# A fixed task table for the attention stage, with other engines for some tasks and the k and v tails in two tiles

## The chip, the cores and the metric

The kernel runs on one core of a Trainium2 chip. A core has five engines that run their own instruction streams and wait for each other through semaphores: TensorE (PE in the profile, with its weight loads as PEld), VectorE (DVE), ScalarE (ACT), GpSimd (POOL) and SyncE (SP). All but a few DMA transfers are issued by SP, in the order of its stream. The metric is the device time of one execution in microseconds (us).

## The reference

Three stages follow each other. The first is attention over B=4, H=8, S=576, D=64 with a second, linear read-out that is mixed in by a gate:

```python
scores = scale * np.matmul(q, k.transpose(0, 1, 3, 2))
scores = np.where(causal, -1000000000.0, scores)
a = np.exp(scores - scores.max(-1, keepdims=True))
a /= a.sum(-1, keepdims=True) + 1e-09
local = np.matmul(a, v)
q_p = phi(q)                      # where(q > 0, q, exp(q) - 1) + 1
mem_out = einsum(q_p, M_prev) / (einsum(q_p, z_prev) + 1e-06)
attn = g * mem_out + (1 - g) * local          # g = sigmoid(beta) per head
```

Then a gated MLP (512 to 1536 and back) and a second MLP (512 to 2048 and back) run over the 2304 tokens. Inputs and outputs are float32.

## The kernel before

Attention is cut into 16 pairs of heads: for each of the 4 batches 4 pairs, each written by one call of `Attention.pair(b, n)`. A pair's rows of q, k and v are four chunks of 128 and a tail of 64 rows. Of a pair, PE transposes k (`tk`, L793), q (`tq`, L804) and the tails of k and q (`tm`, L799); ScalarE or VectorE copy the results out of PSUM (L697, tiles `K` and `S`); PE makes the scores (`s`, L914 and, for the tail rows, L948); VectorE masks them and takes the row minima (L928, L955); ScalarE takes the exponentials (L935, L966); VectorE makes the row factors `r` (L991, L996); GpSimd or VectorE scale the rows (L1007 on GpSimd, L1009 on VectorE, in place in tile `a`); PE transposes them (`t`, L1023, L1045, L1062); they are copied out (tile `R`), and the product `av` (L1087, L1095) ends the pair. Its result goes to DRAM (`xs`, L1121). The read-out of phi(q) runs beside it (`e`, `p`, `nrm`: L822 to L857).

The tails of k and of v of a whole batch lie in one tile, `kv`: v in its partitions 0 to 63, k in 64 to 127, in two buffers, so that one batch's tails can be loaded while the other's are in use. `tm` transposes a whole `kv` block, both halves, and uses the columns that came from k. `av` multiplies a whole `kv` block with a row block whose other half is zero.

Between the pairs stand weight conversions for the next stage (L1160 to L1246) and, from about 85 us on, 24 early products of the gated MLP (`mm`, L1563), for which VectorE and ScalarE need little. PE also runs products on zeros (`idle`, L1517 and L1587), which fill time in which it would wait; there are 9 at the start and 30 (`SPIN`) that are tasks of the plan.

All this is recorded as tasks of a `Plan` with an engine, a cost, what they depend on and which buffers they use. `choose` makes a task with two possible engines; the string `CHOICE` has a digit for each. `order()` then simulates the engines with the costs and takes, on each engine, the ready task with the lowest number in the table `RANK`. The tasks are written in the order that comes out, and each engine's stream is that order with the other engines left out. The simulation makes VectorE and GpSimd wait for each other by rules of its own (`port`, `ends`, `shut`). If a plan has a `table`, `by_table()` is used instead: it lists the tasks in their final order, and costs and rules play no part. The plan of the main stage (`TABLE`) is of that kind already.

The main stage follows on every engine. Its first products (L1749, 144 matmuls) use early tiles `xw`; then come the chains (L1815 and others). It reads `xs` back (`xr`, L1686) and the weight numbers that attention stored (`num`, read at L1327).

Of the kernel before, what the change touches and what calls it, by code (L numbers as in the profile page):

```python
# [19 lines left out]
P = 128  # L20
# [33 lines left out]
    "0100010001010100010001010011110101101010000010010000000000100000000010101011100000011011111010100010"  # L54
    "1100000001010001000000100000010010000101001110011001001010101010110010000101010100101011111010001000"
    "0111010101100000100010100110000111100010100000010101000001011111100001010000100010001000011000110010"
    "0001100001000100011010011000000010001000010100011000001100000010100000010010000000000010100100110000"
    "0010100000101111010100001010000000001010001100101011010111101000001100001111000010100101001011011101"
)
RANK = (  # L60
# [474 lines left out]
def c_tr(n):  # L535
    return 109 * n
# [1647 lines left out]
```

## Time and profile before

| | |
|---|---|
| median of 3 runs | 1011.12 us (1010.63 to 1011.39) |
| the profiled execution | 1011.15 us |
| its span, first to last instruction | 1009.4 us |
| last attention product ends, main stage starts on PE | 247.98 us |
| PE busy over the span | 986.7 us (98%) |
| DVE, ACT, POOL busy over the span | 799.1, 622.9, 129.9 us |
| mean granted TensorE clock | 0.99 of 2.4 GHz |

About 1.75 us of the execution lie outside the span. GpSimd has work in the attention stage alone. A busy PE is not a PE at its peak: the ends of matmuls are modelled, and at half clock it counts as busy too, so the granted clock has to be read beside it.

### The profile page before, as it was taken

The page shows a single profiled execution, that of the slowest core. Times are in us where ns is not written, and L with a number is a line of the kernel's source. Part 1 is how long each engine was busy: PE and PEld are TensorE (multiplying, and loading weights), DVE is VectorE, ACT ScalarE, POOL GpSimd, SP SyncE. Part 2 cuts the span into 40 slices and gives each one's busy share as a digit, 9 for nine tenths or more (in the row PEclk, how much of TensorE's full clock was granted, in tenths as well). Part 3 has the DMA queues.
Part 4 walks back from the last instruction along what each step waited for, and adds up shares of the span by engine and source line. Part 5 has one row for each costly group of instructions (what it writes and reads, how often), then busy time and mean ns, then how long its engine had stood idle before and what let it go on. Part 6 is the DMA issues. An engine that isn't in the chain of part 4 may idle for free.

```text
span 1009.4 us, 17905 instructions
## 1 busy us (share of the span) xinstructions
PE 986.7 (98%) x6546; PEld 929.0 (92%) x6546; DVE 799.1 (79%) x1648; ACT 622.9 (62%) x1287; POOL 129.9 (13%) x170
## 2 busy tenths in 40 slices
PE   7989999999999999999999999999999998999997
PEld 6667777778999999999999999999999998999997
DVE  4989988983888778787768887687788867987983
ACT  4889888863665656656355645577877854454541
POOL 3354657751000000000000000000000000000000
PEclk9989999999999999999999999999999999999999
DMA  8747444222843555657997863125455895544441
GB/s 191 193 117 209 115 123 111 77 73 81 276 134 113 170 178 178 223 187 278 359 348 252 302 225 125 42 88 194 158 193 194 286 343 174 170 155 132 147 135 43
DMA packets 161848, 178.91 MB, mean 177 GB/s; under 512 B 68064, under 2 KB 133088, under 8 KB 161760
## 3 DMA queue, kind: packets, MB, share of 16 engines
q1 hardware_dynamic: 140702, 158.33, 48.6%
q10 hardware_dynamic: 21058, 19.44, 6.3%
q8 instruction: 51, 0.84, 0.3%
q14 instruction: 37, 0.30, 0.1%
HBM read 114.82 MB, written 62.91 MB: 176 GB/s over the span
## 4 chain that ended last, share of the span: by engine, by line
PE 89%; DVE 6%; DMA 2%; ACT 1%; issue 1%; POOL 0%; SPq 0%; ACTq 0%; DVEq 0%
PE mm L1815 39%; PE mm L1990 16%; PE mm L1899 15%; PE av L1095 3%; PE s L914 3%; PE mm L1749 2%; PE t L1045 2%; PE mm L1563 2%; DVE a L928 2%; PE av L1087 1%; PE s L948 1%; DMA rg<-h2s 1%; PE t L1062 1%; PE idle L1587 1%; DMA h2s<-r 1%
## 5 line engine op out<-in xcount | busy, mean ns | idle before, releaser
L1815 PE MATMUL mm<-xw 128*128 128x384 f32 x1944 | 346.4, 334 | 0.6 <-DVE r L1846 0.6
L1815 PEld LDWEIGHTS mm<-xw 128*128 128x128 f32 x1944 | 337.7, 188 | 1.0 <-DVE r L1846 1.0
L1990 PE MATMUL mm<-xw 128*128 128x256 f32 x1296 | 162.6, 284 | 3.1 <-DVE xw L1968 3.1
L1990 PEld LDWEIGHTS mm<-xw 128*128 128x128 f32 x1296 | 159.2, 193 | 3.3 <-DVE xw L1968 3.3
L1899 PE MATMUL mm<-xw 128*128 128x384 f32 x864 | 150.1, 334 | 0.0
L1899 PEld LDWEIGHTS mm<-xw 128*128 128x128 f32 x864 | 149.8, 188 | 0.0
L1967 ACT CAST xw<-rg 128x768 fp32r<-128x768 f32 x72 | 58.5, 833 | 50.5 <-DVE rg L1963 15.1
L935 ACT ACTIVATE a<-a,mn 128x256 f32<-128x256 f32 (+3 forms) x128 | 70.6, 555 | 10.6 <-DVE mn L928 10.3
L1968 DVE TENSOR_TENSOR xw<-rg,xw 128x768 fp32r<-128x768 f32 x72 | 67.4, 952 | 2.4 <-ACT xw L1967 2.3
L1007 POOL TENSOR_SCALAR a<-a,r,one 128x128 f32<-128x128 f32 (+4 forms) x79 | 60.5, 775 | 40.0 <-DVE r L996 20.4
L1815 PE MATMUL mm<-xw,wh 128*128 128x384 f32 x324 | 64.8, 334 | 0.0
L1837 ACT COPY mm<-mm 128x384 f32<-128x384 f32 x54 | 25.1, 465 | 63.7 <-PE mm L1815 63.6
L928 DVE CUSTOM_DVE_ANT_0 a<-s,mask 128x384 f32<-128x384 f32 (+3 forms) x128 | 55.1, 483 | 6.3 <-PE s L914 6.2
L1815 PEld LDWEIGHTS mm<-xw,wh 128*128 128x128 f32 x324 | 56.9, 188 | 0.0
L697 ACT COPY R<-t 128x384 f32<-128x384 f32 (+2 forms) x104 | 47.5, 501 | 15.0 <-PE t L1045 9.5
L1095 PE MATMUL av<-R,vn 128*64 128x320 f32 (+3 forms) x384 | 48.0, 379 | 0.4 <-ACT R L697 0.4
L1095 PEld LDWEIGHTS av<-R,vn 128*64 128x64 f32 x384 | 28.1, 137 | 21.4 <-ACT R L697 1.0
L1698 ACT CAST xw<-h 128x768 fp32r<-128x768 f32 x36 | 29.7, 835 | 28.1 <-DMA h<-hs 17.3
L1701 DVE TENSOR_TENSOR xw<-h,xw 128x768 fp32r<-128x768 f32 x36 | 33.7, 952 | 14.5 <-ACT xw L1698 14.5
L1349 DVE TENSOR_TENSOR wp<-wp 128x256 f32<-128x256 f32 x104 | 42.5, 421 | 1.6
L914 PE MATMUL s<-K,S 64*128 64x256 f32 (+3 forms) x256 | 39.8, 445 | 0.0
L1231 DVE TENSOR_TENSOR xw<-wp,xw 128x768 fp32r<-128x768 f32 x36 | 33.9, 952 | 4.3 <-ACT xw L1229 4.0
(182 smaller groups left out, 1660.7 us busy)
## 6 DMA issues: line engine op xcount, KB each, us to landing
h2s<-r SPq DMA_DIRECT2D x48, 384.0 KB, 3.8
rg<-h2s ACTq DMA_DIRECT2D x72, 256.0 KB, 3.5
park<-pk SPq DMA_DIRECT2D x27, 512.0 KB, 3.0
hs<-h SPq DMA_DIRECT2D x33, 384.0 KB, 5.2
h<-hs SPq DMA_DIRECT2D x33, 384.0 KB, 4.5
xr<-xs SPq DMA_DIRECT2D x24, 384.0 KB, 3.5
rw<-in_moe_w_out_dram SPq DMA_DIRECT2D x16, 512.0 KB, 4.7
rw<-in_moe_w_in_dram SPq DMA_DIRECT2D x16, 512.0 KB, 4.6
```

What stands on the lines that cost most here:

```text
L697: copy(dst(), src())
L914: nc.tensor.matmul(out[h][:, at_[c]:at_[c] + kl[c]], st["S"][halves[h], c * P:(c + 1) * P], st["K"][halves[h], 0:kl[c]], start=True, stop= ...
L928: nc.vector.tensor_tensor_reduce(a, st[f"s{h}{tag}"][:, at_[c]:at_[c] + kl[c]], self.mask0[:, 512 - kl[c]:512], -0.125, 3.0e38, ALU.add, A ...
L935: nc.scalar.activation(a, a, AF.Exp, bias=mn[:, o:o + 1], scale=-1.0, accum_out=sm[:, o:o + 1])
L1007: eng.tensor_scalar(a, a, r, self.one, op0=ALU.mult, op1=ALU.mult)
L1095: nc.tensor.matmul(o[rg][halves[h], c0:c1], V, r, start=False, stop=i == len(terms[rg]) - 1, tile_position=(0, h * 64), skip_group_check=True)
L1349: return lambda: fn(f32(W(o, o + 1)), f32(W(x, x + 1)), f32(W(y, y + 1)))
L1815: nc.tensor.matmul(o, S["k"](k, pw, j), x[k]["at"](px, j), start=begin and not (i or j), stop=j == 1 and i == 2, skip_group_check=True)
L1899: nc.tensor.matmul(o, u["k"](pw, m), h["at"](px, j), start=(p == 0 and j == 0 and n == 0), stop=(p == F1 // 2 - 1 and j == 1 and n == 2), ...
L1967: t = add_act(256 * (b - a), lambda: nc.scalar.copy(dst(j)[:, 0], R(a, b)), deps, [*i_r, i_x[j]])
L1968: return add_dve(256 * (b - a), lambda: nc.vector.tensor_sub(dst(j)[:, 1], R(a, b), f32(dst(j)[:, 0])), [t], [*i_r, i_x[j]])
L1990: nc.tensor.matmul(o, dst(j)[:, px, i, g - 1 - 3 * j], u["k"](w, pw), start=b + i + q == 0 and k in OPEN, stop=b == 3 and i == 1 and q == ...
```

## The change

The attention plan gets a table `FIRST` (1434 numbers, one for each task that is not a transfer in flight) and no `RANK`, so that its order too is written out and nothing is simulated. `CHOICE` has other digits, so some tasks stand on another engine. `kv` with two buffers becomes `kt` (k's tails, zeros in partitions 0 to 63) and `vt` (v's tails, zeros in 64 to 127) with one buffer each; the memory is the same. Three costs and one `port` mark change as well; with a table they decide nothing in this program.

```diff
-    (RANK, 1554 numbers)
+FIRST = (
+    121, 91, 90, 104, 115, 107, 116, 141, 111, 112, 139, 119, 83, 123, 94, 124, 144, 86, 145, 110, 142, 103, 146,
...
 CHOICE = (
-    "0100010001010100010001010011110101101010000010010000000000100000000010101011100000011011111010100010"
+    "1101000111001010000001011101000000000000100011000010010111101100000001001010001000000001101000001010"
...
-        for tags, n in ((("kn", "qn", "vn", "K", "S"), 3), (("zb", "MZ", "a4", "P", "kv", "qz"), 2),
+        for tags, n in ((("kn", "qn", "vn", "K", "S"), 3), (("zb", "MZ", "a4", "P", "qz"), 2), (("kt", "vt"), 1),
...
+        nc.vector.memset(self.kt[0][0:64], 0.0)
+        nc.vector.memset(self.vt[0][64:128], 0.0)
...
-                dma("tails", [690], lambda: tails(self.kv[i_kv.slot], self.k, dn), uses=[i_kv]),
+                dma("tails", [690], lambda: tails(self.kt[i_kt.slot], self.k, dn), uses=[i_kt]),
...
-            held["t_v"] = dma("tails", [690], lambda: tails(self.kv[i_kv.slot], self.v, up), uses=[i_kv])
+            held["t_v"] = dma("tails", [690], lambda: tails(self.vt[i_vt.slot], self.v, up), uses=[i_vt])
...
-            for o, x in (0, self.kv[i_kv.slot]), (128, self.qz[i_qz.slot]):
+            for o, x in (0, self.kt[i_kt.slot]), (128, self.qz[i_qz.slot]):
...
-                            V = st["vn"][:, kc, h] if kc < 4 else self.kv[i_kv.slot][:, n, h]
+                            V = st["vn"][:, kc, h] if kc < 4 else self.vt[i_vt.slot][:, n, h]
...
-                    slow={"PE": (4600, 2)}, turn=TURN, choice=CHOICE, rank=RANK)
+                    slow={"PE": (4600, 2)}, turn=TURN, choice=CHOICE, table=FIRST)
```

The number of instructions of each kind is the same on PE and SP. On VectorE 4 `e<-qn` (L824) and 4 `e<-p,zb` (L836) less stand in the attention stage, and on GpSimd 4 more of each (L822, L836); GpSimd's whole list grows by 18 instructions. In the changed kernel most lines have numbers that are 7 lower (L1749 there is L1742).

**The tails, on SP.** Before, the load of v's tails of the first batch stands behind a weight load and in front of M:

```order
L1160 DMA raw_374<-in_moe_w_gate_dram 128x4x256
L726 DMA kv_0_183<-in_v_dram 64x8x64
L730 DMA MZ_0_187<-in_M_prev_dram 64x4x64 x2
L730 DMA MZ_1_188<-in_M_prev_dram 64x4x64 x2
L711 DMA kn_1_176<-in_k_dram 128x4x64 x2
```

Now, with the v rows of the first pair moved ahead of it:

```order
L704 DMA vn_0_178<-in_v_dram 128x4x64 x2
L723 DMA MZ_0_187<-in_M_prev_dram 64x4x64 x2
L719 DMA vt_0_184<-in_v_dram 64x8x64
L1153 DMA raw_624<-in_moe_w_gate_dram 128x4x256
L704 DMA qn_651<-in_q_dram 128x4x64 x2
```

The load writes `kv_0_183` before and a tile of its own now. **The tails, on PE**, where the fourth tail transpose (`tm`) of the first batch stands. Before:

```order
L948 MATMUL s40_391<-K_294 128x288
L948 MATMUL s41_398<-K_294 128x288
L948 MATMUL s40_404<-K_395 128x288
L799 MATMUL tm_412<-ident_60,kv_0_183 128x128
L799 MATMUL tm_412<-ident_60,qz_0_185 128x128
```

Now:

```order
L856 MATMUL tp_412<-ident_60,p_263 128x128 x4
L859 MATMUL tp4_417<-ident_60,p_263 64x128
L786 MATMUL tk_424<-ident_60,kn_2_177 128x128 x4
L792 MATMUL tm_431<-ident_60,kt_0_183 128x128
L792 MATMUL tm_431<-ident_60,qz_0_185 128x128
```

The transpose reads `kt`, which no load of v writes. **The start, on ACT's queue** (the first pair's second halves of q and k, and q's tail, 128x1x64). Before:

```order
L636 DMA bb_220<-in_beta_dram 128x8
L723 DMA qn_225<-in_q_dram 128x1x64
L711 DMA qn_225<-in_q_dram 128x4x64
L711 DMA kn_0_175<-in_k_dram 128x4x64
L639 ACT_TABLE_LOAD
```

Now:

```order
L629 DMA bb_220<-in_beta_dram 128x8
L704 DMA qn_230<-in_q_dram 128x4x64
L704 DMA kn_0_175<-in_k_dram 128x4x64
L716 DMA qn_230<-in_q_dram 128x1x64
L632 ACT_TABLE_LOAD
```

The tail moved behind the two halves. **The start, on PE**, up to the first scores. Before:

```order
L1517 MATMUL idle_206<-still_131 64x128 x9
L1587 MATMUL idle_240<-still_131 64x128 x11
L804 MATMUL tq_261<-ident_60,qn_225 128x128 x4
L1587 MATMUL idle_240<-still_131 64x128 x5
L793 MATMUL tk_288<-ident_60,kn_0_175 128x128 x4
L1587 MATMUL idle_240<-still_131 64x128 x4
L914 MATMUL s02_301<-K_294,S_274 128x384
```

Now:

```order
L1510 MATMUL idle_206<-still_131 64x128 x9
L1580 MATMUL idle_226<-still_131 64x128 x4
L797 MATMUL tq_234<-ident_60,qn_230 128x128 x4
L786 MATMUL tk_241<-ident_60,kn_0_175 128x128 x4
L1580 MATMUL idle_226<-still_131 64x128 x5
L907 MATMUL s02_265<-K_259,S_253 128x384
```

Eleven of the zero products left this place and stand later. **The second tail block, on PE**: `t4` transposes the scaled tail rows of the second pair that comes to it. Before:

```order
L914 MATMUL s13_768<-K_437,S_645 128x512
L799 MATMUL tm_787<-ident_60,kv_1_184 128x128
L799 MATMUL tm_787<-ident_60,qz_1_186 128x128
L793 MATMUL tk_792<-ident_60,kn_2_177 128x128 x4
L804 MATMUL tq_800<-ident_60,qn_652 128x128 x4
L1023 MATMUL t4_830<-ident_60,a4_0_181 128x128 x4
```

Now:

```order
L907 MATMUL s13_709<-K_353,S_660 128x512
L1580 MATMUL idle_226<-still_131 64x128 x5
L786 MATMUL tk_740<-ident_60,kn_1_176 128x128 x4
L1580 MATMUL idle_226<-still_131 64x128 x4
L797 MATMUL tq_756<-ident_60,qn_748 128x128 x4
L1016 MATMUL t4_761<-ident_60,a4_1_182 128x128 x4
```

Nine zero products stand in this place now. The scaling that `t4` waits for (L1009 of `a4`, 128x576) is the 135th instruction of VectorE's stream before and the 120th now.

## Rows read from the trace of the kernel before

**Rows 1.** The page's head: span, and busy time of each engine.

```profile
span 1009.4 us, 17905 instructions
PE 986.7 (98%) x6546; PEld 929.0 (92%) x6546; DVE 799.1 (79%) x1648; ACT 622.9 (62%) x1287; POOL 129.9 (13%) x170
```

**Rows 2.** Busy time by stretch: us, engines (instructions), granted clock, DMA share, GB/s.

```profile
0.00:25.00 25.00, 19.00 (x119) 15.54 (x120) 12.32 (x45) 10.02 (x28) 9.77 (x31) 0.95 0.89 191
25.00:75.00 50.00, 45.02 (x299) 32.40 (x299) 44.27 (x152) 44.71 (x121) 20.34 (x28) 0.89 0.61 156
75.00:250.00 175.00, 173.14 (x1355) 132.27 (x1352) 144.46 (x482) 133.83 (x388) 99.83 (x112) 1.00 0.41 113
250.00:1009.40 759.40, 749.53 (x4778) 748.80 (x4777) 598.04 (x971) 434.32 (x753) 0.00 (x0) 1.00 0.57 193
```

**Rows 3.** PE's order in time: start, us, line, instructions, idle before.

```profile
14.40 0.33 PE L799 MATMUL tm<-ident,kv 128*128 128x128 f32 x1
...
24.14 0.45 PE L799 MATMUL tm<-ident,kv 128*128 128x128 f32 x1 [5.03 <-DMA kv<-in_v_dram]
```

**Rows 4.** SP's order in time, transfers issued at 17 to 19 us.

```profile
17.56 0.82 SPq L1160 DMA_DIRECT2D raw<-in_moe_w_gate_dram  x1
18.48 0.64 SPq L726 DMA_DIRECT2D kv<-in_v_dram  x1
```

**Rows 5.** Busy time by stretch, in and behind PE's two long waits.

```profile
18.70:23.90 5.20, 0.41 (x2) 0.00 (x0) 1.27 (x8) 1.32 (x4) 0.84 (x2) 0.87 1.21 231
23.90:29.20 5.30, 5.06 (x18) 3.44 (x18) 3.00 (x13) 1.85 (x4) 0.45 (x1) 0.50 0.81 167
50.80:54.60 3.80, 0.29 (x4) 0.06 (x2) 3.80 (x16) 3.80 (x13) 2.42 (x3) 0.82 0.89 190
54.60:60.30 5.70, 5.70 (x23) 5.02 (x24) 4.50 (x18) 3.65 (x10) 1.75 (x3) 0.52 0.33 76
```

**Rows 6.** PE's order in time at the second wait.

```profile
54.59 1.12 PE L1023 MATMUL t<-ident,a 128*128 128x128 f32 x4 [3.51 <-DVE a L1009]
```

**Rows 7.** VectorE: the scaling waited for, and its work up to there by stretch.

```profile
54.02 0.91 DVE L1009 TENSOR_SCALAR a<-a,r 128x576 f32<-128x576 f32 x2
...
0.00:54.60 54.60, 43.62 (x279) 32.31 (x279) 39.35 (x136) 36.95 (x101) 20.46 (x44) 0.93 0.83 193
```

**Rows 8.** The start in time: ACT's queue, then PE.

```profile
1.21 1.15 ACTq L723 DMA_DIRECT2D qn<-in_q_dram  x1
2.39 0.39 ACTq L711 DMA_DIRECT2D qn<-in_q_dram  x1
...
8.25 1.31 PE L1587 MATMUL idle<-still 128*64 128x128 f32 x10
9.49 0.66 PE L793 MATMUL tk<-ident,kn 128*128 128x128 f32 x4
10.07 1.09 PE L1587 MATMUL idle<-still 128*64 128x128 f32 x8
11.09 2.43 PE L914 MATMUL s<-K,S 64*128 64x384 f32 x16
```

**Rows 9.** Groups by line and shape, 0 to 248 us: busy, mean ns, idle before.

```profile
L824 DVE TENSOR_SCALAR e<-qn 128x576 f32<-128x576 f32 x11 | 4.8, 440 | 1.7 <-DMA qn<-in_q_dram 1.7
L836 DVE TENSOR_TENSOR e<-p,zb 128x512 f32<-128x512 f32 x8 | 5.5, 686 | 0.0
L822 POOL TENSOR_SCALAR e<-qn 128x576 f32<-128x576 f32 x5 | 10.7, 2137 | 4.8 <-issue 2.3 <-DVE nrm L844 1.7 <-DMA qn<-in_q_dram 0.8
L836 POOL TENSOR_TENSOR e<-p,zb 128x512 f32<-128x512 f32 x8 | 10.6, 1329 | 22.3 <-DVE nrm L851 12.1 <-DVE p L831 10.1
```

**Rows 10.** VectorE's row factors by shape, 0 to 248 us, and both shapes' spread.

```profile
L991 DVE SCALAR_TENSOR_TENSOR r<-sum,OGP 128x4 f32<-128x4 f32 x16 | 6.3, 392 | 0.9 <-ACT a L935 0.8
L991 DVE SCALAR_TENSOR_TENSOR r<-sum,OGP x32: 147/164/1092, 19.6 to 229.0; 128x4 f32<-128x4 f32 x16, 128x5 f32<-128x5 f32 x16
```

**Rows 11.** PE's order in time where the main stage starts.

```profile
247.98 25.23 PE L1749 MATMUL mm<-xw 128*128 128x384 f32 x144
```

More of the change, by code (lines that the diff above doesn't have):

```diff
@@ L53 @@
 CHOICE = (
-    "0100010001010100010001010011110101101010000010010000000000100000000010101011100000011011111010100010"
[L55 to L58, printed above, removed]
-)
-RANK = (
[76 rows of a table removed]
+    "1101000111001010000001011101000000000000100011000010010111101100000001001010001000000001101000001010"
+    "1010000001001000001000000000101010000000000100000111000011010000111110010000000000010100101110110010"
+    "0001001100010000000110010001000011000011001010101001100010010010100010000001011101010010010000001011"
+    "0101011101000011001000011100001000011000000001011110110000010011101010010101100010010110100000010000"
+    "0010111110101000100011101000011100100001010001000001010011000000010010000001011100100110101111000001"
+)
+FIRST = (
[70 rows of a table added]
 TABLE = (
@@ L303, with __init__ @@
     RELEASE = 90
-    def __init__(self, start=None, over=None, lat=None, slow=None, stay=0, turn=0, keep=False, choice="", rank=(), table=()):
+    def __init__(self, start=None, over=None, lat=None, slow=None, stay=0, turn=0, keep=False, choice="", table=()):
         self.slow, self.stay, self.turn, self.keep = slow or {}, stay, turn, keep
@@ L309, in __init__ @@
         self.tasks, self.caps, self.taken, self.start = [], {}, {}, start or {}
-        self.choice, self.chosen, self.rank, self.table = choice, 0, rank, table
+        self.choice, self.chosen, self.table = choice, 0, table
         self.opened = None
@@ L322, in add @@
     def add(self, eng, dur, prio, fn, deps=(), uses=(), lat=0, behind=None, port=False, form=0, by=None):
-        if self.rank:
-            prio = self.rank[len(self.tasks)]
         t = {"eng": eng, "port": port, "form": form, "dur": dur + (self.over.get(eng, 0) if self.over else 0), "prio": (prio, len(self.tasks)), "fn": fn, "uses": list(dict.fromkeys(uses)),
@@ L615, in __init__ @@
         self.a4 = [ac.tile([P, 640], F32, name=f"a4_{i}") for i in range(2)]
-        self.kv, self.qz, self.MZ = (
-            [ac.tile([P, NP, 2, D], F32, name=f"{x}_{i}") for i in range(2)] for x in ("kv", "qz", "MZ"))
+        self.kt, self.vt, self.qz, self.MZ = (
+            [ac.tile([P, NP, 2, D], F32, name=f"{x}_{i}") for i in range(n)]
+            for x, n in (("kt", 1), ("vt", 1), ("qz", 2), ("MZ", 2)))
+        nc.vector.memset(self.kt[0][0:64], 0.0)
+        nc.vector.memset(self.vt[0][64:128], 0.0)
         self.one = ac.tile([P, 1], F32, name="one")
@@ L620, in __init__ @@
         for i in range(2):
-            nc.vector.memset(self.kv[i][0:64], 0.0)
             for h in range(2):
@@ L732, in pair @@
         if n == 0:
-            self.batch = {"z": pl.inst("zb"), "M": pl.inst("MZ"), "k": pl.inst("kv"), "q": pl.inst("qz")}
+            self.batch = {"z": pl.inst("zb"), "M": pl.inst("MZ"), "k": pl.inst("kt"), "v": pl.inst("vt"), "q": pl.inst("qz")}
         held = self.batch
-        i_z, i_M, i_kv, i_qz = (held[x] for x in "zMkq")
+        i_z, i_M, i_kt, i_vt, i_qz = (held[x] for x in "zMkvq")
         i_K, i_S, i_P = pl.inst("K"), pl.inst("S"), pl.inst("P")
@@ L809, in pair @@
         t_tk = add("PE", c_tr(4), "tk", tk, l_k, [i_k, i_tk, i_K])
-        t_tm = add("PE", c_tr(2), "tm", tm, t_kt, [i_kv, i_qz, i_tm, i_K])
+        t_tm = add("PE", c_tr(2), "tm", tm, t_kt, [i_kt, i_qz, i_tm, i_K])
         t_tq = add("PE", c_tr(4), "tq", tq, l_q[:2], [i_q, i_tq, i_S])
@@ L866, in tp @@
             nc.tensor.transpose(t[0:64, 0:128], p[:, 8], self.ident)
-        t = choose("min", [("POOL", c_pool(576) + 60, lambda: f_min(nc.gpsimd), False),
+        t = choose("min", [("POOL", 2080, lambda: f_min(nc.gpsimd), False),
                            ("DVE", c_dve(576), lambda: f_min(nc.vector), True)], l_q, [i_q, i_e])
@@ L996, in f_inv @@
                 nc.vector.reciprocal(r, r)
-            t = add("DVE", 80, f"sum{h}", f_sum, [t_exp[x] for x in keys] + [self.gated], [i_mn])
+            t = add("DVE", 80, f"sum{h}", f_sum, [t_exp[x] for x in keys] + [self.gated], [i_mn], True)
             return add("DVE", 94, f"sum{h}", f_inv, [t], [i_mn])
@@ L1100, in av @@
             t_av = add("PE", c_two(*cols), "av0", f, deps + t_P + [l_v, t_vt, t_M],
-                       [*i_o, i_P, i_v, i_M, i_kv, *i_R0, i_R1, i_x], form=2)
+                       [*i_o, i_P, i_v, i_M, i_vt, *i_R0, i_R1, i_x], form=2)
             out = []
@@ L1204, in number @@
                                ("DVE", c_dve(512), lambda: size_of(nc.vector), True)], [t], [i_raw, i_F])
-        t2 = plan.add("ACT", c_act(512) + 40, prio, tail, [t], [i_raw, i_L])
+        t2 = plan.add("ACT", c_act(512) + 100, prio, tail, [t], [i_raw, i_L])
         t = plan.add("DVE", c_dve(512), prio, clamp, [t], [i_F], port=True)
```

145 rows, old and new, of tables (FIRST, RANK) are left out of this document.

## The prediction

> **What bounds the kernel now.** I read the page first, then the stretches, then PE's order in time around the gaps that the stretches show. PE is busy for 986.7 of 1009.4 us [rows 1]: it is the bound over the span, and the other engines have room on average. So a change of order can only win where PE waits or runs at half clock. The stretches say where [rows 2]. From 250 us on PE is busy 749.53 of 759.40 us at full clock, and there the change touches nothing. From 75 to 250 us it is busy 173.14 of 175 at clock 1.00. What is left lies in the first 75 us: 64.02 busy of 75, at clock 0.95 and 0.89. The attention stage ends at 247.98 us [rows 11], and PE works on from there at once, so each us that attention ends earlier is a us of the whole, as long as the main stage finds its inputs.
>
> PE's order in time shows two long waits. The first, 5.03 us, ends at 24.14 with the landing of a transfer from v [rows 3], and the instruction that waited is a transpose of the k tails: it reads the whole of `kv`, and v's half is written by a load issued only at 18.48, behind a weight load [rows 4]. The reader is to see that the other engines stand too: in those 5.20 us VectorE is busy 1.27, ScalarE 1.32, GpSimd 0.84 [rows 5]. The second wait, 3.51 us, is of another kind: PE waits for a scaled block from VectorE [rows 6], and VectorE and ScalarE are busy for all 3.80 us of it [rows 5]. VectorE simply had too much ahead of that block: 39.35 us of work in 136 instructions by 54.6 us [rows 7]. After each wait the granted clock is 0.50 and 0.52, that is the lower level, 1.2 GHz, for 5.30 and 5.70 us [rows 5].
>
> **The change part by part.** The sum is made against the profiled execution's own 1011.15 us, with 1.75 of it outside the span; the median, 1011.12, is the same for this purpose.
>
> *The tails in two tiles.* With `kt` the transpose reads nothing that a load of v writes; its own load, k's tails, is the one that the three earlier `tm` needed as well. So the 5.03 us go, and with them the half clock behind them: 5.30 x (1 - 0.50) = 2.65 us. Together 7.7. Since every engine stood in that wait, all of them move forward and none becomes the limit by it. Bounds: nothing, if another late transfer stands there (bytes in front of it are the same), and 7.7. I take 7.7, because three transposes of the same k tails ran from 14.40 us on without a wait [rows 3].
>
> *The start.* On ACT's queue q's tail, whose issue takes 1.15 us from 1.21 on, moves behind the halves of q and k; q's half was issued at 2.39 [rows 8] and now takes its place: 2.39 - 1.21 = 1.18 us earlier. On PE `tk` follows `tq` directly, without the zero products that stood from 8.25 to 9.49: 1.24 us. First scores, at 11.09 before, come 2.4 us earlier. The zero products that leave this place stand in later gaps. Bounds: nothing (the copy of K now stands on VectorE behind `e<-qn`, which needs the tail that is now issued last) and 3.4 (1.02 us of zero products, 10.07 to 11.09, gone as well). I take 2.4.
>
> *The second wait.* Ahead of the scaling that PE waits for stand 120 VectorE instructions, and 135 before. At the mean of that stretch, 39.35 / 136 = 0.29 us, the 15 are 4.3 us, more than the 3.51 of the wait; those that left are rather the long ones (`e<-p,zb` takes 0.69 [rows 9]). So the wait goes, and the half clock behind it: 3.51 + 5.70 x (1 - 0.52) = 6.2 us. But nine zero products now stand between the scores and `t4`. Four of them took 1.02 us from 10.07 on [rows 8], so nine cost 2.3 us, whether PE had to wait or not. 6.2 - 2.3 = 3.9. Bounds: -2.3 (the wait stays and the zero products come on top) and 6.2 (the zero products only fill time that PE would have waited anyway). I take 3.9.
>
> *Work moved to GpSimd.* Four `e<-qn` cost GpSimd 4 x 2.137 = 8.5 us and give VectorE back 4 x 0.440 = 1.8. Four `e<-p,zb` cost 4 x 1.329 = 5.3 and give back 4 x 0.686 = 2.7 [rows 9]. The other 10 of its 18 new instructions cost about 0.76 each (129.9 us in 170 instructions), 7.6. Together 21.4 us more on GpSimd. I take this at nothing: GpSimd is busy 129.9 us of the 250 [rows 1, 2], and before `e<-p,zb` alone it stood idle 22.3 us for VectorE's results [rows 9]. The cover is that idle time; if it is gone, the price is up to 21.4.
>
> *One buffer for each tail.* The next batch's `vt` can be loaded only when the last `av` of the batch before has read it, and SP issues in order, so the transfers behind it wait too: the next q, k and v rows, and the stores of `x`. `av` of the next batch waits for the load. Issue and landing took from 18.48 to about 24.1, 5.6 us, when the queue was full [rows 3, 4]. Three changes of batch: bounds nothing and 3 x 5.6 = 17. I take nothing: later the DMA share is 0.41 against 0.89 at the start [rows 2], and between two batches' `av` stand score products and transposes of other pairs.
>
> *The rest.* PE does the same instructions. From 75 us on it has at most 175 - 173.14 = 1.9 us to win [rows 2]; I take nothing. The last `num` store moves to the end of attention. What hides that is the first block of the main stage, 25.23 us [rows 11], which needs no `num`; without that cover it would cost a store and a load.
>
> Sum: 7.7 + 2.4 + 3.9 = 14.0. 1011.15 - 14.0 = **997.2 us**.
>
> **The rivals.** *Only the tail's wait goes.* VectorE and ScalarE were busy for all of the second wait, so with everything 7.7 us earlier they may make PE wait again elsewhere; a new wait of 3.5 us with half clock behind it costs the 6.2 us that the second term counts on, and the start is then no gain, since PE arrives early at the same full engines. Then 1011.15 - 7.7 = 1003.5. For it: VectorE 44.27 and ScalarE 44.71 of 50 us busy [rows 2]. Against it: 15 instructions fewer ahead of the one place where it shows.
>
> *GpSimd becomes what PE waits for, and it gets slower.* The place is the first 75 us, where six of the first pair's nine scalings now stand on GpSimd (four before) and a block's transpose waits for them. The price is up to 21.4 us on the path: 1011.15 - 14.0 + 21.4 = 1018.6. It decides when more than 14.0 of the 21.4, two thirds, lie on the path. For it: VectorE and GpSimd hold each other up. The row factors, a few elements wide, take 164 ns as a rule and up to 1092, and 392 as the mean of one shape [rows 10], so 16 x (392 - 164) = 3.6 us are lost in that group alone. Against it: GpSimd was busy 30.1 of the first 75 us [rows 2]. The Trainium skill's page SBUF — State Buffer, section Who interferes with whom, has a rule of this kind: a VectorE instruction with two SBUF inputs and a GpSimd instruction that reads SBUF exclude each other, and the one that starts second waits for the whole of the other. The trace agrees with it in the 147 to 1092 ns of one instruction [rows 10]. By that rule every added GpSimd instruction can hold VectorE for its own length, which is this rival's 21.4 us in full.
>
> *It is given back, or does nothing.* The main stage's first x pieces come from the last pairs' `xs`, and if transfers rather than PE set its start, or if three late `vt` loads cost 14 us, the time stays at 1011. Against it: PE waited for nothing at 247.98 [rows 11], and those loads hang on the last `av`, which moves with the rest.
>
> **How the numbers follow.** My forecast (990.5 to 1001.5) gets 0.62: its terms are read from waits that are there, but the second rests on a place that I can only count out. Only the tail (1001.5 to 1008) 0.22; no change 0.06; slower 0.10. The forecast's low end is 14.0 + 2.3 (zero products free) + 1.0 (start) + 1.9 (after 75 us) = 19.2 better, 992, less 1.5 for small waits that are not counted: 990.5. The range is 990.5 to 1006: it takes in most of the first rival, and leaves out its end and the last two, less than 2 in 10. About 0.2%, 2 us, is what a measurement here can tell from no change. Faster 0.84, same 0.06, slower 0.10.
>
> **What would show it.** In the profile after, the tail transposes wait for no load of v; the first scores start near 8.7 us; PE's wait for VectorE at the second `t4` is under 1 us; the granted clock of 25 to 75 us is above 0.95; and the main stage's first product (L1742 there) starts near 234 us and takes 25 us again, with the same 761 us behind its start as before (1009.4 - 247.98). It is wrong if new waits of PE with half clock behind them stand between 10 and 75 us, if they end with GpSimd's scalings (the slower rival), if `av` waits for `vt`, or if the main stage takes longer than 761 us.

## The result and the profile after

The changed kernel takes 994.16 us (median of 4, 993.47 to 995.31), the kernel before took 1010.88 in the same comparison: a ratio of 0.984 (95% interval 0.982 to 0.986), 16.7 us less. The prediction was 997.2, so its sum of 14.0 was 2.7 us short. The profiled execution took 995.31 us, the longest of the four.

First the page's head and the stretches (length, then for each engine busy us and its instructions, PE's granted clock, DMA share, GB/s), against [rows 1, 2]:

```profile
span 993.5 us, 17912 instructions
...
PE 980.3 (99%) x6546; PEld 925.3 (93%) x6546; DVE 799.1 (80%) x1638; ACT 620.1 (62%) x1279; POOL 154.4 (16%) x188
```

```profile
0.00:25.00 25.00, 23.66 (x150) 18.64 (x151) 18.37 (x69) 15.42 (x42) 15.07 (x37) 1.00 0.76 181
25.00:75.00 50.00, 49.62 (x404) 36.88 (x403) 48.77 (x155) 47.94 (x137) 45.45 (x46) 1.00 0.63 164
75.00:232.00 157.00, 155.95 (x1212) 119.75 (x1211) 133.68 (x445) 121.46 (x347) 93.90 (x107) 1.00 0.45 120
232.00:993.50 761.50, 751.11 (x4786) 750.06 (x4784) 598.31 (x971) 435.28 (x755) 0.00 (x0) 1.00 0.58 193
```

The second row is the one to look at. From 25 to 75 us PE was busy 45.02 of 50 at clock 0.89 and is now busy 49.62 at 1.00. VectorE (44.27 before, 48.77 now) and ScalarE (44.71, now 47.94) are nearly full, and GpSimd has gone from 20.34 to 45.45. Not one engine was relieved in this stretch; all four were filled.

PE's order in time at the places of [rows 3, 6, 8, 11] (start, duration, engine and line, out<-in, count, and in brackets the idle time ahead and what ended it):

```profile
6.71 0.80 PE L797 MATMUL tq<-ident,qn 128*128 128x128 f32 x4
7.34 0.60 PE L786 MATMUL tk<-ident,kn 128*128 128x128 f32 x4
7.87 1.30 PE L1580 MATMUL idle<-still 128*64 128x128 f32 x10
9.55 2.43 PE L907 MATMUL s<-K,S 64*128 64x384 f32 x16 [0.37 <-ACT e L820]
...
29.08 0.76 PE L1080 MATMUL av<-P,MZ 128*64 128x320 f32 x4
...
37.49 1.31 PE L1580 MATMUL idle<-still 128*64 128x128 f32 x10
38.73 0.66 PE L786 MATMUL tk<-ident,kn 128*128 128x128 f32 x4
39.31 1.09 PE L1580 MATMUL idle<-still 128*64 128x128 f32 x8
40.33 0.66 PE L797 MATMUL tq<-ident,qn 128*128 128x128 f32 x4
40.82 0.60 PE L1016 MATMUL t<-ident,a 128*128 128x128 f32 x4
...
50.61 0.76 PE L1080 MATMUL av<-P,MZ 128*64 128x320 f32 x4
```

```profile
231.39 25.12 PE L1742 MATMUL mm<-xw 128*128 128x384 f32 x144
```

There is no wait at the second `t4` (40.82; 54.59 before), only zero products ahead of it, and the tail transposes (one group over their four calls, 13.1 to 20.2 us) have no wait either:

```profile
L792 PE MATMUL tm<-ident,kt x4: 272/272/328, 13.1 to 20.2; 128*128 128x128 f32 x4
```

How the lead grows can be read from the attention products: the first `av` starts at 29.08 (40.18 before: 11.1 us earlier), the second at 50.61 (68.22: 17.6), the main stage at 231.39 (247.98: 16.6). Behind that start stand 762.1 us (993.5 - 231.39), 761.4 before. So all of it is won by 50 us, and 1.7 us less of it are there at the end.

Where PE's time went up to the main stage is read from two rows, the changed kernel's and then that of before:

```profile
0.00:231.39 231.39, 228.62 (x1759) 174.66 (x1760) 200.83 (x667) 184.44 (x524) 154.41 (x188) 1.00 0.52 137
0.00:247.98 247.98, 235.14 (x1758) 178.19 (x1758) 200.22 (x676) 187.72 (x533) 129.94 (x170) 0.97 0.50 130
```

PE was idle for 2.8 us (231.39 - 228.62) and for 12.8 before: 10.1 us less. It was busy for 6.5 us less, of which the two stretches of half clock in [rows 5] explain 2.65 + 2.74 = 5.4. So 15.5 of the 16.6 us are PE's waits and the half clock behind them.

### The profile page after: what moved, and what is told of

It is laid out like the page before. It is cut to its first block, busy times and chain, and to the rows that moved or that the text cites. A ratio compares the mean times of both kernels' runs of the same rounds, so it can differ in the third digit from the quotient of the medians.

```text
span 993.5 us, 17912 instructions
## 1 busy us (share of the span) xinstructions
PE 980.3 (99%) x6546; PEld 925.3 (93%) x6546; DVE 799.1 (80%) x1638; ACT 620.1 (62%) x1279; POOL 154.4 (16%) x188
## 4 chain that ended last, share of the span: by engine, by line
PE 88%; DVE 5%; DMA 4%; ACT 1%; issue 1%; POOL 0%; ACTq 0%; SPq 0%; DVEq 0%; POOLq 0%
PE mm L1808 37%; PE mm L1983 17%; PE mm L1892 15%; PE av L1088 3%; PE s L907 3%; PE mm L1742 3%; PE mm L1556 2%; PE t L1038 2%; DMA rg<-h2s 2%; DVE a L921 1%; PE av L1080 1%; PE s L941 1%; PE t L1055 1%; DMA raw<-in_moe_w_out_dram 1%; DVE a L1002 1%
## 5 line engine op out<-in xcount | busy, mean ns | idle before, releaser
L928 ACT ACTIVATE a<-a,mn 128x512 f32<-128x512 f32 (+3 forms) x128 | 71.1, 558 | 12.9 <-DVE mn L921 12.0
L1000 POOL TENSOR_SCALAR a<-a,r,one 128x128 f32<-128x128 f32 (+4 forms) x85 | 67.5, 806 | 51.7 <-DVE r L989 19.9
L921 DVE CUSTOM_DVE_ANT_0 a<-s,mask 128x512 f32<-128x512 f32 (+3 forms) x128 | 56.0, 483 | 4.7 <-PE s L907 4.4
L1691 ACT CAST xw<-h 128x768 fp32r<-128x768 f32 x36 | 29.6, 834 | 27.6 <-DMA h<-hs 17.6
L690 ACT COPY R<-t 128x384 f32<-128x384 f32 (+2 forms) x90 | 40.2, 502 | 5.8 <-PE t L1038 2.3
```

The source lines that it names most:

```text
L690: copy(dst(), src())
L921: nc.vector.tensor_tensor_reduce(a, st[f"s{h}{tag}"][:, at_[c]:at_[c] + kl[c]], self.mask0[:, 512 - kl[c]:512], -0.125, 3.0e38, ALU.add, A ...
L928: nc.scalar.activation(a, a, AF.Exp, bias=mn[:, o:o + 1], scale=-1.0, accum_out=sm[:, o:o + 1])
L1000: eng.tensor_scalar(a, a, r, self.one, op0=ALU.mult, op1=ALU.mult)
```

## The experiments

The runs take the prediction's terms one at a time. The rivals are its own, and one more: that the order and the engines are worth something only together.

**The first wait, by the place of one load.** In `late_tail` the kernel before has its own order written out as a table, with task 135, the load of v's tails of the first batch, moved:

```diff
- ... 41, ... 135, ... 137, ... 297, ... 133, 155, ...
+ ... 41, ... 137, ... 297, ... 133, 135, 155, ...
```

> The kernel before, with its order and engines written out as a table so that nothing is simulated, and one task moved: the load of v's tails of the first batch is issued behind the load of the first pair's v rows, that is behind all four tail transposes. The tile kv stays one tile, so if the 5.03 us wait falls it falls by the place of the load alone. My account of the first wait (5.03 of waiting and 2.65 of half clock behind it): 1010.9 - 7.7 = 1003.2 us, the fourth tail transpose with no wait for kv. If only the wait goes and the clock behind it stays low: 1005.9. Rival, PE then waits as long at the next place because VectorE and ScalarE are full: 1008 to 1011.

1003.56 us, ratio 0.993 (0.992 to 0.995): 1010.9 x 0.0067 = 6.8 us. That is also the time of the rival by which only the tail's wait goes (1003.5). The first `av` starts at 32.55, 7.6 us earlier. PE's time line shows the second wait untouched, 7.5 us earlier than in [rows 6]:

```profile
47.12 1.12 PE L1052 MATMUL t<-ident,a 128*128 128x128 f32 x4 [3.50 <-DVE a L1038]
```

So the first term is nearly right in size (6.8 to 7.6 of 7.7), and it reaches the end: PE did not get a longer wait for it elsewhere. But it needed no second tile. `new_order_one_tile` asks the other way round:

```diff
-        for tags, n in ((("kn", "qn", "vn", "K", "S"), 3), (("zb", "MZ", "a4", "P", "qz"), 2), (("kt", "vt"), 1),
+        for tags, n in ((("kn", "qn", "vn", "K", "S"), 3), (("zb", "MZ", "a4", "P", "kv", "qz"), 2),
...
-                dma("tails", [690], lambda: tails(self.kt[i_kt.slot], self.k, dn), uses=[i_kt]),
+                dma("tails", [690], lambda: tails(self.kv[i_kv.slot], self.k, dn), uses=[i_kv]),
...
-            held["t_v"] = dma("tails", [690], lambda: tails(self.vt[i_vt.slot], self.v, up), uses=[i_vt])
+            held["t_v"] = dma("tails", [690], lambda: tails(self.kv[i_kv.slot], self.v, up), uses=[i_kv])
```

> The changed kernel, with the tails of k and v in one tile kv of two buffers again, order and engines as in the changed kernel. In the new list the load of v's tails stands behind the fourth tail transpose, so if the place of the load is what counts the wait doesn't come back: 993.5 to 995 us. If the two tiles themselves are worth the first term, 994.2 + 5 to 7.7 = 999 to 1002 with a wait of the tail transposes for a load of v. If the single buffers of kt and vt cost something in the changed kernel, 992 to 994.

993.38 us, 0.983 (0.982 to 0.985): the same as the changed kernel. SP's order in time shows what happens to the shared tile:

```profile
17.58 1.38 SPq L722 DMA_DIRECT2D MZ<-in_M_prev_dram  x2
20.16 0.60 SPq L718 DMA_DIRECT2D kv<-in_v_dram  x1
```

In the new table the load stands behind the fourth `tm`, which PE starts at 19.86 in this run, so now the load waits for the transpose: SP stands from 18.96 to 20.16, 1.2 us, and PE for nothing. In the old order the load stood ahead of that transpose and PE waited 5.03 us for it. In the new order the two tiles (and their single buffers) are worth nothing that can be measured here; the place of the load is enough for the whole term. Two tiles in the old order were not run.

**The start, alone.** `late_tail_start` is `late_tail` with the two edits of the start:

```diff
- 119, ... 116, ... 112, ... 141, ... 109, ... 96, ... 105, 82, ... 95, 139, 87, ...
+ ... 116, ... 112, 119, ... 141, 139, ... 109, ... 96, ... 105, 82, ... 95, 87, ...
```

(119 is q's tail on ScalarE's queue, 116 and 112 the halves of q and k, 141 `tq`, 139 `tk`, those between them zero products.)

> The kernel before with the v tail's load late (the run late_tail, 1003.6 us) and with the two edits of the start alone: on ScalarE's queue the load of q's tail moves behind the halves of q and k, and tk follows tq directly on PE, the five zero products between them moving behind tk. Engines as before. By my second term the first scores come 2.4 us earlier than 11.6 and the whole as well: 1001.2 us; with the 1.5 us that the changed kernel's trace shows: 1002.1. Rival (the start is no gain because PE meets the same full VectorE and ScalarE later): first scores earlier by 1.5 to 2.4, but the wait at the second t4, 3.50 us in late_tail, grows by as much, and the time stays at 1003.6.

1002.64 us, 0.993 (0.992 to 0.995): no gain over `late_tail` (0.993) that can be told. First scores start at 10.36 (11.21 in `late_tail`, where the expectation has 11.6), the first `av` at 31.65 (32.55), the second `t4` at 46.30 (47.12), but the second `av` at 60.20 (59.52): a lead of 0.8 us became a loss of 0.7. The wait is the same 3.50 us in both, so it did not grow by the lead, as the rival had it; what differs is the clock behind it. Stretches of `late_tail`, and then of `late_tail_start`:

```profile
47.10:49.10 2.00, 1.98 (x9) 1.98 (x10) 2.00 (x10) 1.13 (x5) 0.00 (x0) 0.50 1.03 275
49.10:51.10 2.00, 2.00 (x10) 1.56 (x10) 0.98 (x5) 1.62 (x3) 1.75 (x3) 0.75 0.87 195
```

```profile
46.30:48.30 2.00, 2.00 (x10) 2.00 (x11) 2.00 (x10) 1.14 (x5) 0.00 (x0) 0.50 0.72 188
48.30:50.30 2.00, 2.00 (x6) 1.32 (x6) 0.94 (x4) 1.58 (x3) 1.75 (x3) 0.50 0.75 171
50.30:52.30 2.00, 2.00 (x11) 2.00 (x10) 1.80 (x6) 1.23 (x3) 0.00 (x0) 0.50 0.75 202
```

3.0 us at the lower level there (0.50 for 2.0, and 0.75, half of it, for 2.0), 6.0 here: 3.0 x 0.5 = 1.5 us, which is the 0.8 and the 0.7. But each trace is one execution, and this difference lies within what executions of one kernel show. The four of `late_tail` had mean granted clocks of 0.996, 0.993, 0.996 and 0.994, the five of `late_tail_start` 0.993 four times and 0.996; the traces happen to be of a 0.996 (1002.26 us, the fastest) and a 0.993. So it is not shown that the edit of the start lengthens the half clock (the last section has the same difference where no edit is). What is shown is that a lead of 0.8 us reaches the second `t4` in full. What it brings to the end is open: 0.9 us by the medians, 0.2 by the ratios, and the intervals are wider than either.

`k_first` is the changed kernel with one swap in `FIRST`, the copy of K (142) ahead of `e<-qn` (145) on VectorE:

```diff
- ... 144, 86, 145, 110, 142, 103, 146, ...
+ ... 144, 86, 142, 110, 145, 103, 146, ...
```

> The changed kernel with one swap on VectorE: the first copy of K stands ahead of the first e<-qn, which waits for q's tail until 8.34 us. My prediction named this order as the reason for which the start term could be less than 2.4. First scores then start at 8.7 to 9.0 us, not 9.55; if that goes through, 993.4 to 993.7 us; if VectorE's and ScalarE's later work sets the pace, 994.2, with the time given back before the first av at 29.08.

992.64 us, 0.983 (0.982 to 0.985): not to be told from the changed kernel. First scores start at 9.60, since in this run `tk` waited 1.33 us for k's half to land and started at 7.81 only. From `tk` to the scores are 1.79 us, 2.21 in the changed kernel (7.34 to 9.55): the swap gives 0.4 us there, and the landing took it. Whether 0.4 us would carry is not decided by this run.

**The second wait.** `late_tail_weights` takes 2.2 us of VectorE work (tasks 5 to 8, a weight conversion) from ahead of the scaling that `t4` waits for (task 348) to behind it; the ScalarE and GpSimd tasks 9 and 10 and the next load 21 follow.

```diff
- ... 5, ... 6, ... 7, ... 8, ... 884, 348, 343, ...
+ ... 884, 348, 5, 6, 7, 8, 21, 9, 10, 343, ...
```

> The kernel before with the v tail's load late (1003.6 us) and with four VectorE instructions of a weight conversion, 2.2 us together, moved from ahead of the scaling that the second t4 waits for to behind it, with the ScalarE and GpSimd instructions and the load that follow from them. PE's work and the engines are the same. If VectorE's backlog alone makes the 3.50 us wait: the wait falls to about 1.3, the half clock behind it becomes short or goes (up to 2.7), and the time is 998.7 to 1001.4. If ScalarE's exponentials are as late as VectorE: the wait stays over 2.5 us and the time is 1002.5 to 1003.6. If the moved work is missed at the next place: 1003.6 or more with a new wait behind 50 us.

1004.36 us, 0.995 (0.993 to 0.996): no gain over `late_tail`; the intervals overlap (0.993 to 0.995), so a small loss if anything. The wait is split:

```profile
45.72 0.76 PE L1052 MATMUL t<-ident,a 128*128 128x128 f32 x4 [2.41 <-DVE a L1038]
48.37 1.11 PE L1074 MATMUL t<-ident,a 128*128 128x128 f32 x4 [1.67 <-DVE a L1038]
```

2.41 us and 1.67, together 0.6 more than 3.50: the moved work now stands ahead of the next scaling, and the next transpose waits for that. Here, taking work from ahead of one block to behind it did not take the wait away: VectorE was full.

`no_zeros` leaves out the nine zero products ahead of the second `t4` in the changed kernel.

```diff
-            plan.add("PE", 214, None, spin, (), [i_idle])
+            plan.add("PE", 214, None, (lambda: None) if len(plan.tasks) in LESS else spin, (), [i_idle])
```

> The changed kernel without the nine zero products that stand between the scores and the second t4 (nothing in their place; the result is the same). As my third term has it, they cost 2.3 us: 994.2 - 2.3 = 991.9 us. Rival, they fill time in which PE waits for VectorE anyway: 994.2, with a wait of some 2 us in their place, or, if the granted clock then falls, 994 to 997.

994.63 us, 0.985 (0.983 to 0.987): no gain. PE waits in their place, and its clock doesn't fall:

```profile
40.35 0.66 PE L1017 MATMUL t<-ident,a 128*128 128x128 f32 x4 [1.59 <-DVE a L1003]
```

```profile
40.35:42.50 2.15, 2.15 (x14) 1.79 (x15) 2.01 (x8) 2.15 (x9) 2.15 (x4) 1.00 1.04 247
```

The second `av` starts at 50.78, 50.61 in the changed kernel. In this place the zero products cost nothing that can be measured, and after a wait of 1.59 us they weren't needed for the clock either.

**Order and engines apart.** `old_order_new_engines` is the kernel before in its own order with the changed `CHOICE`; `new_order_old_engines` the changed kernel with the old `CHOICE`.

> The order of the kernel before, with the engines (CHOICE) of the changed kernel, and kv as one tile: 219 of the 500 choices are the other engine. If the new engines are worth the second wait by themselves (15 fewer VectorE instructions ahead of it): 1010.9 - 3.9 to 6.2 = 1004.7 to 1007.0, with the 5.03 us wait at the fourth tail transpose still there. Rival, the engines are fitted to their order and to no other: new waits in 10 to 75 us, 1011 to 1025.

> The changed kernel (its order, its two tail tiles) with the engines of the kernel before. If the order and the tiles carry the tails (7.7) and the start (1.5) and the engines carry the second wait and what follows: 994.2 + 6.5 = 1000.7 us, with more VectorE work ahead of the second av. If the order carries nearly all: 994 to 996. Rival, the order is fitted to its engines: over 1005. If GpSimd's added work were a cost in the changed kernel: under 994.

1029.07 us, 1.018 (1.016 to 1.020), and 1066.14, 1.055 (1.053 to 1.057). Each half alone makes the kernel slower than it was before, by 18 and 55 us. They exchange 219 choices each, those between ScalarE and VectorE too, so two smaller runs exchange only the 25 early tasks whose engine changed between VectorE and GpSimd, in the changed kernel (`new_early_back`) and in `late_tail` (`late_tail_early_gp`). (19 of the 25 stand on GpSimd in the changed kernel and on VectorE before, 6 the other way round.)

> The changed kernel, its order as it is, with the 25 early tasks (up to the 340th of the order) whose engine changed between VectorE and GpSimd put back where the kernel before had them: 19 return to VectorE, 6 leave it, so 13 x 0.29 = 3.8 us more on VectorE and some 10 us less on GpSimd in the first 50 us. The choices between ScalarE and VectorE stay as changed. If GpSimd's early work is what makes room on VectorE and with it the 9 us that neither the tail nor the start gives: 998 to 1004. If the order alone gives it: 993.5 to 996. If GpSimd's work costs VectorE as much as it relieves it (they hold each other up): 991 to 994.

> The kernel before with the v tail's load late (1003.6 us), its order as it is, with the same 25 early tasks on the engines of the changed kernel: VectorE relieved by 13 x 0.29 = 3.8 us, GpSimd with some 10 us more. If relief of VectorE is the matter by itself: the 3.50 us wait at the second t4 goes, 997.5 to 1001. If the engines pay only in an order that puts GpSimd's tasks early enough: 1003 to 1012, with PE waiting for GpSimd's scalings.

| | old early engines | new early engines |
|---|---|---|
| old order, v's tail late | 1003.56, 0.993 (0.992 to 0.995) | 1007.40, 0.998 (0.997 to 0.999) |
| new order | 1009.13, 0.999 (0.998 to 1.000) | 994.16, 0.984 (0.982 to 0.986) |

In the old order the new engines of these 25 tasks cost 4 us, in the new order they are worth 15. The other 194 choices matter as much or more: with the old engines for them too, the new order takes some 57 us more (1066.14 - 1009.13). The longest waits of PE between 25 and 75 us, in `new_early_back` and then in `late_tail_early_gp`:

```profile
32.18 0.90 PE L1055 MATMUL t<-ident,a 128*128 128x128 f32 x3 [4.23 <-POOL a L1000]
45.57 0.63 PE L856 MATMUL tp<-ident,p 128*128 128x128 f32 x4 [2.68 <-DVE p L850]
```

```profile
43.67 0.66 PE L892 MATMUL tp<-ident,p 128*128 128x128 f32 x4 [2.62 <-POOL p L886]
52.73 0.66 PE L1052 MATMUL t<-ident,a 128*128 128x128 f32 x4 [2.33 <-DVE a L1038]
```

In both PE comes to blocks that are not ready, GpSimd's as well as VectorE's. GpSimd's order in time ahead of the first of these waits and of the third shows why:

```profile
29.49 1.26 POOL L829 TENSOR_TENSOR e<-p,zb 128x512 f32<-128x512 f32 x1 [2.72 <-DVE p L824]
...
31.23 0.89 POOL L1000 TENSOR_SCALAR a<-a,r,one 128x128 f32<-128x128 f32 x1
```

```profile
40.20 2.29 POOL L851 TENSOR_SCALAR e<-qn 128x576 f32<-128x576 f32 x1
42.47 1.15 POOL L886 TENSOR_TENSOR p<-p,nrm 128x576 f32<-128x576 f32 x1
```

In `new_early_back` the scaling that PE needs (31.23) stands behind two read-out tasks, and the first of these waited 2.72 us for a `p` that VectorE makes only from 28.66 to 29.41. In `late_tail_early_gp` the `p` that PE needs (42.47) stands directly behind 2.29 us of `e<-qn`. VectorE has room there (busy 41.21 us from 25 to 75 us, 47.29 in `late_tail`), and PE waits all the same. So at these waits the block that PE needs next stands too far behind in an engine's list. That this is the whole of the 4 and the 15 us is not shown.

**What GpSimd's and VectorE's work costs now.** `gp_double` and `dve_double` are the changed kernel with instructions written twice, with the same result.

```diff
+                for _ in range(2 if num in (3, 4) else 1):          # gp_double, GpSimd's e<-qn
                     eng.tensor_scalar(e, st["qn"], 0.0, 1.0, op0=ALU.min, op1=ALU.mult)
...
+            for _ in range(2 if num in (0, 1, 2, 3, 4) else 1):     # dve_double, VectorE's p<-qn,e
                 nc.vector.scalar_tensor_tensor(p, st["qn"], 0.0, st["e"], op0=ALU.max, op1=ALU.add)
```

> The changed kernel with GpSimd's e<-qn written twice in the fourth and the fifth pair (the same values again): 2 x 2.14 = 4.3 us more on GpSimd by 45 us, nothing else changed. My prediction took GpSimd's added 21.4 us at nothing because it has idle time. If that cover is still there: 993.5 to 995.5 us. If GpSimd now sets PE's pace in this stretch (busy 45.4 of 50 us there), up to 4.3 us: 996 to 998.5, with waits of PE, VectorE or the other engines for GpSimd's results. If GpSimd's instructions hold VectorE for their whole length as well: 998.5 or more.

> The changed kernel with VectorE's p<-qn,e written twice in the first five pairs (the same values again): 5 x 0.65 = 3.2 us more on VectorE by 60 us, nothing else changed. If VectorE's backlog is what PE waits for (busy 48.8 of 50 us): 996 to 997.5. If PE's own work and its nine filling zero products leave room: under 995.5, up to 1.6 us being taken by the zero products' time. If ScalarE or GpSimd sets the pace: 993.5 to 995.

997.61 us, 0.988 (0.986 to 0.989), and 996.45, 0.987 (0.986 to 0.989). The second `av` starts at 53.67 and 53.34, that is 3.1 and 2.7 us later than in the changed kernel, for what was meant as 4.3 us more on GpSimd and 3.2 on VectorE. In `gp_double` the longest wait for GpSimd is VectorE's:

```profile
32.84 0.30 DVE L838 TENSOR_REDUCE nrm<-e 128x9 f32<-128x144 f32 x1 [2.62 <-POOL e L841]
```

The added time itself came out longer. In `gp_double` the two double instructions took 4.54 and 5.02 us, the single ones of the changed kernel 2.14 each, so 5.3 us more and not 4.3. Of these 3.1 reach the path: GpSimd's work is not hidden in the changed kernel. In `dve_double` too: its five double instructions took 9.41 us together, the five single ones of the changed kernel 4.29, so 5.1 us more and not 3.2. Here are all of its kind in `dve_double`, then the fourth double one, and last what GpSimd did beside it:

```profile
L825 DVE SCALAR_TENSOR_TENSOR p<-qn,e x11: 741/758/1711, 9.7 to 66.6; 128x576 f32<-128x576 f32 x11
...
36.01 2.49 DVE L825 SCALAR_TENSOR_TENSOR p<-qn,e 128x576 f32<-128x576 f32 x2
...
36.23 1.65 POOL L1183 TENSOR_TENSOR wA<-wA,wL 128x512 int32<-128x512 int32 x1 [0.68 <-DVE wA L1174]
```

The second of the two started at 36.8 and took 1.71 us, where 0.74 is the shortest of its kind. That is 1 us more, and GpSimd's instruction beside it (the last row) ended at 37.88, 1.1 us after that start. Of the 5.1 us, 2.7 reach the second `av`.

## Why the prediction was right, and where it was not

The forecast (faster, 997.2, range 990.5 to 1006) held. Of its marks, no wait of the tail transposes, no wait at the second `t4`, a clock above 0.95 and some 761 us (762.1) behind the start of the main stage are there; first scores came at 9.55, not 8.7, and the main stage at 231.4, earlier than 234. By its steps:

*The tails, 7.7: right in the wait and nearly in size, not in what removes it.* 6.8 us by the time and 7.6 by the first `av` (`late_tail`). The step said that the wait goes because `kt` is another tile; with one tile in the new order it is gone as well. That the load comes behind the transposes in the table is enough.

*The start, 2.4: over-sized.* First scores are 1.54 us earlier. The bound named for it is what the trace shows: the first `e<-qn` stands until 8.34 for a transfer (the profile names a load of q's tail rows; of what `e<-qn` reads, q's tail is issued last), and K's copy behind it starts at 8.72. VectorE's order in time:

```profile
8.34 0.46 DVE L817 TENSOR_SCALAR e<-qn 128x576 f32<-128x576 f32 x1 [2.97 <-DMA qz<-in_q_dram]
8.72 0.68 DVE L690 COPY K<-tk 128x512 f32<-128x512 f32 x1
```

In the old order 0.85 us of earlier scores and 0.9 at the first `av` came of the two edits (`late_tail_start`). By the first `av` the changed kernel is 11.1 us ahead and `late_tail` 7.6, 3.5 us more. What lies ahead of that `av`, in the changed kernel and then in `late_tail`:

```profile
0.00:29.08 29.08, 27.74 (x180) 22.11 (x180) 22.45 (x84) 19.50 (x52) 18.83 (x40) 1.00 0.78 184
0.00:32.55 32.55, 31.02 (x201) 24.09 (x202) 24.33 (x90) 22.07 (x59) 16.13 (x39) 1.00 0.85 197
```

PE is busy for 3.3 us less there and waits 0.2 less. Most of that is the nine zero products that now stand behind this `av`: at the prediction's own price 2.3 us. (In `late_tail` all 30 stand ahead of it, in the changed kernel 21.) The prediction counted part of their leaving in its second term (1.24), another part only in that term's bounds (1.02), and charged nine of them in its third. No run moves them alone.

*The second wait, 3.9: under-sized.* From the first `av` to the second the changed kernel takes 21.5 us and the kernel before 28.0, 6.5 less, and the wait with its half clock was 6.2. The step that failed is the 2.3 us for nine zero products "whether PE had to wait or not": they fill time that PE would have waited anyway (`no_zeros`: second `av` at 50.78 without them, 50.61 with them), which was the term's own upper bound, 6.2.

*The account.* 7.6 + 3.5 + 6.5 - 1.0 (between the second `av` and the main stage) - 0.7 (in the main stage) = 15.9, the difference of the spans, where the prediction had 7.7 + 2.4 + 3.9 = 14.0. That the sum came this near is in part luck: the first term was over-sized by up to 0.9, the start's two edits brought 0.9 of 2.4, and the 2.3 that was charged for the zero products was not owed. The 1.0 is no wait but work that stands later in the new order. Between the second `av` and the main stage PE is busy for 179.35 of 180.78 us and was for 177.90 of 179.76, so it is idle for 1.4 us now and was for 1.9. The 0.7 is no sign of the change: from the start of the main stage to the end the other traces, whose main stage is the same, show 759.5 to 762.4 us.

*Why the wait goes: the reason given was a part.* The prediction counted 15 VectorE instructions fewer ahead of the scaling, that is relief of VectorE. Relief in the old order (`late_tail_early_gp`) cost 4 us, and moving work behind the block (`late_tail_weights`) gained nothing. The table of four shows that it takes both: these tasks on the new engines, and an order made for them.

*GpSimd for nothing: the step that was wrong in kind.* Idle time of 22.3 us before one instruction type [rows 9] was taken as cover. That is right for the kernel before and wrong for the changed one, which has used it up: 45.45 of 50 us busy, and 5.3 us more delayed the second `av` by 3.1. The rival that GpSimd becomes a limit was thus half true: it is one, but in the new order the new engines of the 25 tasks are worth 15 us in all. Its other half, that GpSimd and VectorE hold each other up, is seen in single instructions (1.71 us for 0.74 in `dve_double`) but has not grown into a loss that these rows show: the row factors take 162 ns as a rule and 505 at most (1092 before, [rows 10]), and `gp_double` cost less than the length of what was added (3.1 of 5.3).

```profile
L984 DVE SCALAR_TENSOR_TENSOR r<-sum,OGP x32: 148/162/505, 14.8 to 218.6; 128x4 f32<-128x4 f32 x16, 128x5 f32<-128x5 f32 x16
```

How long VectorE stands beside GpSimd differs. Here are a row factor of the kernel before and a `p<-qn,e` of the changed one, each behind the GpSimd instruction beside it:

```profile
99.86 1.15 POOL L857 TENSOR_TENSOR p<-p,nrm 128x576 f32<-128x576 f32 x1
99.93 1.09 DVE L991 SCALAR_TENSOR_TENSOR r<-sum,OGP 128x4 f32<-128x4 f32 x1
...
17.43 2.14 POOL L815 TENSOR_SCALAR e<-qn 128x576 f32<-128x576 f32 x1
17.58 1.12 DVE L824 SCALAR_TENSOR_TENSOR p<-qn,e 128x576 f32<-128x576 f32 x1
```

The first pair ends together, at 101.0 us. In the second VectorE loses 0.4 us (1.12 for 0.74) and ends 0.9 us ahead of GpSimd. By the rule of the Trainium skill (SBUF — State Buffer, Who interferes with whom), that a VectorE instruction with two SBUF inputs and a GpSimd instruction that reads SBUF exclude each other, the second standing for the whole of the first, all of GpSimd's added time could fall on VectorE. The trace agrees with it in the first pair and not in the second; in full, over the kernel, it would have made the rival's 1018.6 us, and 994.2 were measured.

*Single buffers for nothing: right.* One tile with two buffers gives the same time (993.38 us, `new_order_one_tile`). The `num` store was not tried by itself; PE starts the main stage with no wait at 231.39.

## What to carry to other kernels

Which of the two waits in a shared tile, the transfer or its reader, follows from which is written first: 5.03 us of PE here one way round, 1.2 us of SP and nothing of PE the other. Before splitting a tile, see whether another place for the load is enough. Ask of each lead which wait it meets next, and test it by that edit alone. Here leads of 7.6 and 0.8 us both passed a wait of 3.50 us without its growing. Where two traces differ behind a wait, look first at how far executions of one kernel differ. And where a table sets both the order and the engines, neither can be judged alone: idle time of an engine is worth something only if its results come when they are needed.

## What was not expected of the hardware

The same wait of 3.50 us, ended by the same instruction, was followed by 3.0 us at the lower clock level in the traced execution of `late_tail` and by 6.0 in that of `late_tail_start`, whose program differs only at the start; in the kernel before it was nearly all of 5.70 us (clock 0.52, [rows 5]). So what follows a wait varied by 1.5 us with the same wait. That no edit is needed for it can be seen in the main stage, where the code is the same in all kernels and PE waits some 3 us for `xw`. Here are 20 us around that wait in the changed kernel (a wait of 3.52 us), in `no_zeros` (3.22) and in `dve_double` (3.0):

```profile
820.00:840.00 20.00, 17.56 (x134) 17.56 (x135) 16.91 (x30) 9.63 (x16) 0.00 (x0) 0.91 0.45 151
820.00:840.00 20.00, 19.03 (x136) 19.03 (x137) 17.03 (x30) 9.08 (x15) 0.00 (x0) 0.83 0.41 132
820.00:840.00 20.00, 16.41 (x133) 15.85 (x133) 14.53 (x26) 8.39 (x14) 0.00 (x0) 1.00 0.56 184
```

At half clock for the lower level, 0.91 is 3.6 us of it, 0.83 is 6.8 and 1.00 none: the shorter of the first two waits was followed by twice as much. After the wait of 1.59 us in `no_zeros` the clock stayed at 1.00.
